# Sign of the converted weights in ScalarE's pass, and one accumulation for the first two units of layer 1

## The chip, the cores and the metric

One NeuronCore of a Trainium2 chip runs the whole program. It has five engines with a queue each: TensorE (PE, with its weight loads as PEld), VectorE (DVE), ScalarE (ACT), GpSimd (POOL) and SyncE (SP), which here only issues transfers. Each engine works through its instructions in the order in which they stand. TensorE reads its operands from SBUF and writes to PSUM, of which there are eight banks of 128 partitions by 512 float32 values. The metric is the device time of one execution in microseconds (us); less is better.

## The reference, cut to what matters

```python
def _attn_ref(q, k, v):                    # (4, 8, 576, 64) each; causal, window of 64
    scores = np.where(mask, scale * np.matmul(q, k.transpose(0, 1, 3, 2)), -1e9)
    attn = np.exp(scores - max); attn = attn / (sum + 1e-09)
    return np.matmul(attn, v)
x = attn_out.transpose(0, 2, 1, 3).reshape(2304, 512)
h = np.maximum(x @ w_in1, 0.0);  x = h * h @ w_out1        # layer 1: 512 -> 2048 -> 512
h = x @ w_in2;                   out = h * np.cos(h) @ w_out2   # layer 2, same sizes
```

The weights of both layers come into the kernel as float64 (their words are seen as pairs of int32), everything else is float32.

## The kernel before, in words

**Products in three parts.** Every float32 operand of the two layers is split into a high and a low part in a type that TensorE multiplies at full rate, and every product is the sum of three: high by high, high by low, low by high. That is why all matmuls of the layers come in groups of three per block of 128 rows, and in groups of twelve for four blocks.

**Units and slices.** The 2304 tokens are cut into nine blocks of 256. Layer 1 works on units: blocks 0, 1 and 2 are units of 256 tokens each, blocks 3 and 4, 5 and 6, 7 and 8 are units of 512 (`spans`, line 415). The 2048 hidden features are cut into 16 slices of 128. An *item* is one unit and one slice: `g1` (line 825) makes the hidden slice in PSUM (tile `ph`, 12 matmuls), `UnitA.act` (line 593) applies relu and square and splits the result (tile `g`: relu, square and square again on ACT, the subtraction on DVE), and `g2` (line 621) adds the slice's share to the unit's output (tile `accA`, 12 matmuls) two items later (`LAG`). So TensorE alternates: `ph` of item i, `accA` of item i-2, `ph` of item i+1, and so on. A matmul's moving operand has as many columns as the unit has tokens, 256 or 512. The outputs leave PSUM through a small ring of two buffers (`x2`) and go to DRAM; layer 2 (`UnitB`, 512 tokens a unit) reads them back.

**Start.** TensorE's first work is attention for block 0, since unit 0 needs its result as input `X`; attention for later blocks is spread between the items. In one group of attention, TensorE makes the scores (`S`), DVE masks and takes the maximum (`mm`, L484), ACT takes the exponential (`pb`, L490), DVE normalises (L496, L497, L500), TensorE transposes (`T`), ACT or DVE copies (`PT`, or `pb` itself in the group of block 1 that borrows a weight buffer), TensorE multiplies by the values (`O`), and ACT and DVE split the result into `X` (L557, L560). Units 0 and 1 are run in turns, item by item, with unit 1 two slices behind (lines 807 to 810), so that a new slice of weights is needed only every second item.

**Converting a slice of weights** (`convert_w`, line 264) turns 128 by 1024 float64 values into float32: ACT scales the high words as if they were float32 (`c0`, by 2^-112) and the low words (`c1`); DVE shifts the high words left by three bits (`c2`, L298), puts the sign bit in (`c3`, L301), and adds the low words (`c4`, L306). For layer 1, ACT then makes the high part (`c5`) and DVE the low part (`c6`, L327), and the slice can be used. For layer 2 the float32 result is stored to DRAM (`w2_dram`) while layer 1 runs, and is read back and split later.

**What sets the order.** All work is recorded as operations with a key, the engines that may do it, a cost on each, and what it depends on. `Plan.run` (line 103) is a list scheduler: it gives out operations engine by engine in the order of its own estimated times (keys break ties within 0.03 us), also choosing the engine where two are allowed, and the instructions are written in that order. Only the order survives; on the chip the queues run at the chip's speed. A changed cost or key therefore can move instructions anywhere behind it. Transfers are issued by SP, in its own planned order.

The lines that the change touches are 283 to 315 (conversion), 415 (`spans`), 621 to 630 (`g2`), 804 to 816 (the list of items and the items at which attention is recorded), 885 (the key's position `pos`) and 915.

Of the kernel before, what the change touches and what calls it, by code (L numbers as in the profile page):

```python
# [9 lines left out]
F32 = mybir.dt.float32  # L10
# [169 lines left out]
def kernel(  # L180
# [83 lines left out]
    def convert_w(src, j, key, after=None, dst=None, early=None):  # L264
# [3 lines left out]

        nm = f"{src.tensor.name}_{j}"
# [14 lines left out]
        def c0(e):  # L284
            hw = words()[1].bitcast(F32)
            copy(e, hw, hw, 2.0**-112)
# [13 lines left out]
        def c3(e):  # L300
            nc.vector.scalar_tensor_tensor(  # L301
                s["w"], words()[1], -(1 << 31), s["w"], ALU.bitwise_and, ALU.bitwise_or)

# [10 lines left out]
        o3 = op({"DVE": dve_us(2 * DM)}, key, c3, [o2], use=[rb, tb])  # L314
        o4 = op({"DVE": dve_us(2 * DM)}, key, c4, [o3, o1], use=[rb, tb])
# [99 lines left out]
    spans = [(0, 1), (1, 1), (2, 1)] + [(n, 2) for n in range(3, NUA, 2)]  # L415
# [158 lines left out]
    class UnitA:  # L574
# [46 lines left out]
        def g2(self, j, m, t, w):  # L621
            i, k = divmod(m, self.per)
            if j == 0 and k == 0:
                self.acc[i] = ps_acc.tile(
                    [P, self.per, self.w], F32, tag="acc", name=f"accA_{self.n}_{i}")
            for p, (wl, gl) in enumerate(((0, 0), (0, 1), (1, 0))):
                nc.tensor.matmul(  # L627
                    self.acc[i][:, k, :], w[:, 1, wl, m * P:m * P + P], t["g"][:, gl, :],
                    start=(j == 0 and p == 0 and k == 0),
                    stop=(j == NJ - 1 and p == 2 and k == self.per - 1), skip_group_check=True)  # L630
# [7 lines left out]
        def finish(self, key, ends):  # L638
            for i, b_acc in enumerate(self.acc_b):
# [18 lines left out]
                for n in self.parts:  # L658
                    for c in range(c0, c0 + self.per):
                        x2_done[n, c] = o  # L660

# [145 lines left out]
    items = [(units[0], j) for j in range(SK)]  # L807
    for j in range(NJ - SK):
        items += [(units[0], SK + j), (units[1], j)]
    items += [(units[1], j) for j in range(NJ - SK, NJ)]  # L810
    items += [(u, j) for u in units[2:] for j in range(NJ)]
    NA = NSA * NJ
    att_at = {0: [1], 2 * NJ - SK: [2], 2 * NJ: [3, 4]}
    for s in range(3, NSA - 1):
        n, k = spans[s + 1]
        att_at[s * NJ] = list(range(n, n + k))
# [67 lines left out]
    for i in range(len(items) + LAG + 1):  # L884
        pos = float(i - LAG)
# [25 lines left out]
        if d >= 0 and i != NA + LAG:  # L911
            g2(d, pos, gs.pop(d))
            k, odd = divmod(d - (NA - NJ), 2)
            if 0 <= k < NJ // 2 and odd:
                reload_w2(k, NA - NJ + 2.4 * k, w2_done[2 * k] + w2_done[2 * k + 1] + [gate])
# [64 lines left out]
```

## Time and profile before

| | |
|---|---|
| three runs, median (lowest to highest) | 894.70 us (893.42 to 894.98) |
| the profiled execution, its own time | 894.97 us |
| its span, first to last instruction | 893.2 us |
| PE busy | 867.7 us of the span, 5424 matmuls |
| DVE, ACT busy | 546.0 us, 474.8 us |
| the part before the last matmul of `accA` for item 1 | 53.44 us |

The profiled execution took 894.97 us, 1.77 us more than its span. An engine's busy time counts a matmul to its modelled end, so that two back-to-back matmuls overlap in the list; the spacing of their starts is what TensorE spends on each. The column PEclk is the clock that TensorE was granted: 1.00 is 2.4 GHz, 0.50 is 1.2 GHz.

### The profile page before, as it was taken

The page shows a single profiled execution, that of the slowest core. Times are in us where ns is not written, and L with a number is a line of the kernel's source. Part 1 is how long each engine was busy: PE and PEld are TensorE (multiplying, and loading weights), DVE is VectorE, ACT ScalarE, POOL GpSimd, SP SyncE. Part 2 cuts the span into 40 slices and gives each one's busy share as a digit, 9 for nine tenths or more (in the row PEclk, how much of TensorE's full clock was granted, in tenths as well). Part 3 has the DMA queues.
Part 4 walks back from the last instruction along what each step waited for, and adds up shares of the span by engine and source line. Part 5 has one row for each costly group of instructions (what it writes and reads, how often), then busy time and mean ns, then how long its engine had stood idle before and what let it go on. Part 6 is the DMA issues. An engine that isn't in the chain of part 4 may idle for free.

```text
span 893.2 us, 13884 instructions
## 1 busy us (share of the span) xinstructions
PE 867.7 (97%) x5424; PEld 741.5 (83%) x5424; DVE 546.0 (61%) x1182; ACT 474.8 (53%) x980; POOL 5.0 (1%) x25
## 2 busy tenths in 40 slices
PE   5699999999999999999999999999999999999998
PEld 4499999998788878888888888888888888888897
DVE  4999956644454345433644976667656666766665
ACT  6979977666556566554434533343334433433444
POOL 2000000000000000000000000000000000000000
PEclk8789999999999999999999999999999999999999
DMA  8753234523533254314542200020002000200010
GB/s 333 295 208 150 72 125 157 184 95 122 192 137 130 75 189 151 139 71 142 176 154 95 72 24 0 1 84 12 1 0 83 12 1 0 71 1 1 8 41 23
DMA packets 23169, 85.43 MB, mean 96 GB/s; under 512 B 2368, under 2 KB 4416, under 8 KB 19008
## 3 DMA queue, kind: packets, MB, share of 16 engines
q1 hardware_dynamic: 23104, 84.55, 26.3%
q8 instruction: 42, 0.69, 0.3%
q14 instruction: 23, 0.19, 0.1%
HBM read 66.72 MB, written 17.83 MB: 95 GB/s over the span
## 4 chain that ended last, share of the span: by engine, by line
PE 91%; DVE 4%; ACT 3%; DMA 1%; issue 1%; SPq 0%; ACTq 0%; DVEq 0%
PE ph L837 42%; PE accB L771 22%; PE accA L627 20%; PE S L471 2%; PE O L522 2%; PE T L508 2%; ACT raw_in_w_dram L245 1%; DMA raw_in_w_dram<-in_w_dram 1%; DVE cw_in_w_dram L301 1%; DVE W_in_w_dram L327 1%; DVE pb L484 0%; DVE pb L500 0%; ACT W_in_w_dram L245 0%; DMA qk<-in_qk_dram 0%; ACT g L604 0%
## 5 line engine op out<-in xcount | busy, mean ns | idle before, releaser
L837 PE MATMUL ph<-X,W_in_w_dram 128*128 128x256 f32 (+1 forms) x1152 | 225.0, 343 | 1.6 <-DVE W_in_w_dram L327 1.6
L627 PE MATMUL accA<-g,W_in_w_dram 128*128 128x256 f32 (+1 forms) x1152 | 222.1, 339 | 0.0
L837 PE MATMUL ph<-X,W 128*128 128x512 f32 (+1 forms) x960 | 209.8, 368 | 0.0
L771 PE MATMUL accB<-W,gb 128*128 128x512 f32 x864 | 208.8, 390 | 0.0
L837 PEld LDWEIGHTS ph<-X,W_in_w_dram 128*128 128x128 f32 x1152 | 182.0, 192 | 26.7 <-DVE W_in_w_dram L327 2.1
L627 PEld LDWEIGHTS accA<-g,W_in_w_dram 128*128 128x128 f32 x1152 | 180.9, 191 | 23.2 <-issue 0.7
L837 PEld LDWEIGHTS ph<-X,W 128*128 128x128 f32 x960 | 169.3, 188 | 31.2
L771 PEld LDWEIGHTS accB<-W,gb 128*128 128x128 f32 x864 | 161.0, 188 | 32.9 <-ACT gb L748 0.2
L721 ACT ACTIVATE u<-ph,quarter 128x512 f32<-128x512 f32 (+1 forms) x80 | 51.7, 646 | 148.8 <-PE ph L837 148.8
L613 DVE TENSOR_TENSOR g<-r,g 128x256 fp32r<-128x256 f32 (+1 forms) x96 | 53.1, 555 | 94.3 <-ACT r L608 93.8
L725 DVE TENSOR_SCALAR u<-u 128x512 f32<-128x512 f32 (+1 forms) x80 | 32.0, 400 | 121.2 <-ACT u L721 121.2
L604 ACT ACTIVATE g<-r 128x256 fp32r<-128x256 f32 (+1 forms) x96 | 50.4, 525 | 77.8 <-PE accA L627 77.3
L748 ACT ACTIVATE gb<-rr 128x512 fp32r<-128x512 f32 (+1 forms) x80 | 47.2, 590 | 83.6 <-DVE rr L743 83.6
L600 ACT ACTIVATE r<-ph 128x256 f32<-128x256 f32 (+1 forms) x96 | 46.5, 484 | 54.5 <-PE ph L837 54.2
L245 ACT ACTIVATE raw_in_w_dram<-raw_in_w_dram 128x1024 f32<-128x1024 f32 x64 | 72.8, 1158 | 3.7 <-DMA raw_in_w_dram<-in_w_dram 3.7
L490 ACT ACTIVATE pb<-pb,mm 128x128 f32<-128x128 f32 x144 | 55.9, 390 | 16.4 <-DVE mm L484 16.4
L740 ACT ACTIVATE u<-rr,hpi 128x512 f32<-128x512 f32 (+1 forms) x80 | 53.7, 672 | 0.3 <-DVE rr L736 0.2
L729 DVE SCALAR_TENSOR_TENSOR rr<-u,ph 128x512 f32<-128x512 f32 (+1 forms) x80 | 50.7, 634 | 2.5
L743 DVE TENSOR_TENSOR rr<-ph,u 128x512 f32<-128x512 f32 (+1 forms) x80 | 50.4, 630 | 1.4 <-ACT u L740 1.3
L751 DVE TENSOR_TENSOR gb<-rr,gb 128x512 fp32r<-128x512 f32 (+1 forms) x80 | 50.5, 631 | 1.0 <-ACT gb L748 1.0
L733 DVE SCALAR_TENSOR_TENSOR rr<-u,rr 128x512 f32<-128x512 f32 (+1 forms) x80 | 50.4, 630 | 0.3
L608 ACT ACTIVATE r<-r 128x256 f32<-128x256 f32 (+1 forms) x93 | 48.8, 524 | 3.0
(61 smaller groups left out, 541.9 us busy)
## 6 DMA issues: line engine op xcount, KB each, us to landing
raw_in_w_dram<-in_w_dram SPq DMA_DIRECT2D x32, 1024.0 KB, 7.3
qk<-in_qk_dram SPq DMA_DIRECT2D x18, 576.0 KB, 4.5
v<-in_v_dram SPq DMA_DIRECT2D x18, 512.0 KB, 3.6
w_dram<-cw_in_w_dram SPq DMA_DIRECT2D x16, 512.0 KB, 3.1
w<-w_dram SPq DMA_DIRECT2D x8, 1024.0 KB, 4.8
x_dram<-x SPq DMA_DIRECT2D x18, 256.0 KB, 2.4
out_dram<-o SPq DMA_DIRECT2D x18, 256.0 KB, 2.0
xr<-x_dram SPq DMA_DIRECT2D x16, 256.0 KB, 2.7
```

Source lines behind the costliest of these rows:

```text
L245: nc.scalar.activation(o, i, AF.Copy, scale=scale)
L490: nc.scalar.activation(t["pb"][:, e, r, i], t["pb"][:, e, r, i], AF.Exp, bias=t["mm"][:, e, r, i:i + 1], scale=-1.0, accum_out=t["sm"][:, ...
L604: nc.scalar.activation(t["g"][:, 0], t["r"], AF.Square)
L613: nc.vector.tensor_tensor(t["g"][:, 1], t["r"], f32(t["g"][:, 0]), ALU.subtract)
L627: nc.tensor.matmul(self.acc[i][:, k, :], w[:, 1, wl, m * P:m * P + P], t["g"][:, gl, :], start=(j == 0 and p == 0 and k == 0), stop=(j == ...
L721: nc.scalar.activation(t["u"], ph()[:, 0:w], AF.Identity, bias=quarter, scale=INV_2PI)
L729: nc.vector.scalar_tensor_tensor(t["r"], t["u"], -C1, ph()[:, 0:w], ALU.mult, ALU.add)
L733: nc.vector.scalar_tensor_tensor(t["r"], t["u"], -C2, t["r"], ALU.mult, ALU.add)
L740: nc.scalar.activation(t["u"], t["r"], AF.Sin, bias=hpi)
L751: nc.vector.tensor_tensor(t["g"][:, 1], t["r"], f32(t["g"][:, 0]), ALU.subtract)
L771: nc.tensor.matmul(self.acc[m], t["g"][:, gl, m * P:m * P + P], w[:, 1, wl], start=(j == 0 and k == 0), stop=(j == NJ - 1 and k == 2))
L837: nc.tensor.matmul(t["ph"][:, 0:u.w], wb.tile[:, 0, wl, c * P:c * P + P], u.x(xl, c), start=(c == 0 and k == 0), stop=(c == NCC - 1 and k ...
```

## The change

The scaling pass on ACT (`c0`) becomes a parametric rectifier: positive words are multiplied by 2^-112 as before, negative ones by 2^-112 times -2^32. A negative word thus becomes a positive float32 whose exponent is larger by 32; 32 is bit 5 of the exponent field, that is bit 28 of the word, and the shift by three of `c2` moves it to bit 31, where the sign belongs. `c3` on DVE is left out. This holds for the 16 slices of either layer.

The first two blocks become one unit of 512 tokens, `(0, 2)`. For slices 0 to 5 it is worked by two halves of 256 columns in turns, as units 0 and 1 were (`Half`, items 0 to 11); both halves add into the two ranges of columns of the same four PSUM banks. Slices 6 to 15 (items 12 to 21) are done for 512 tokens at once. There are 22 items where there were 32. Each item's position for the keys is now in the list `place`, since items no longer stand one unit of position apart.

```diff
         def c0(e):
             hw = words()[1].bitcast(F32)
-            copy(e, hw, hw, 2.0**-112)
+            nc.scalar.activation(hw, hw, AF.Prelu, scale=2.0**-112, alpha=-(2.0**32))
...
-        def c3(e):
-            nc.vector.scalar_tensor_tensor(
-                s["w"], words()[1], -(1 << 31), s["w"], ALU.bitwise_and, ALU.bitwise_or)
...
-        o3 = op({"DVE": dve_us(2 * DM)}, key, c3, [o2], use=[rb, tb])
-        o4 = op({"DVE": dve_us(2 * DM)}, key, c4, [o3, o1], use=[rb, tb])
+        o4 = op({"DVE": dve_us(2 * DM)}, key, c4, [o2, o1], use=[rb, tb])
...
-    spans = [(0, 1), (1, 1), (2, 1)] + [(n, 2) for n in range(3, NUA, 2)]
+    spans = [(0, 2), (2, 1)] + [(n, 2) for n in range(3, NUA, 2)]
...
-            if j == 0 and k == 0:
+            if j == 0 and k == 0 and self.n > 0:
...
-                    start=(j == 0 and p == 0 and k == 0),
+                    start=(j == 0 and p == 0 and k == 0 and self.n > 0),
...
+    class Half:
+        w = UA
+        groups = NCC
+        group_us = 3 * pe_us(UA)
+
+        def __init__(self, unit, k):
+            self.unit, self.k = unit, k
+            self.act = lambda *a: UnitA.act(self, *a)
+
+        def x(self, hl, c):
+            return self.unit.x(hl, c)[:, self.k * UA:self.k * UA + UA]
...
+        def g2(self, j, m, t, w):
+            acc, first = self.unit.acc, j == 0 and self.k == 0
+            if first:
+                acc[m] = ps_acc.tile([P, 1, 2 * UA], F32, tag="acc", name=f"accA_{self.unit.n}_{m}")
+            for p, (wl, gl) in enumerate(((0, 0), (0, 1), (1, 0))):
+                nc.tensor.matmul(
+                    acc[m][:, 0, self.k * UA:self.k * UA + UA],
+                    w[:, 1, wl, m * P:m * P + P], t["g"][:, gl, :],
+                    start=(first and p == 0), stop=False, skip_group_check=True)
...
-    items = [(units[0], j) for j in range(SK)]
-    for j in range(NJ - SK):
-        items += [(units[0], SK + j), (units[1], j)]
-    items += [(units[1], j) for j in range(NJ - SK, NJ)]
-    items += [(u, j) for u in units[2:] for j in range(NJ)]
-    NA = NSA * NJ
-    att_at = {0: [1], 2 * NJ - SK: [2], 2 * NJ: [3, 4]}
-    for s in range(3, NSA - 1):
+    J0 = 6
+    halves = [Half(units[0], k) for k in range(2)]
+    items = [(halves[0], j) for j in range(SK)]
+    for j in range(J0 - SK):
+        items += [(halves[0], SK + j), (halves[1], j)]
+    items += [(halves[1], j) for j in range(J0 - SK, J0)]
+    place = [float(i) for i in range(2 * J0)]
+    items += [(units[0], j) for j in range(J0, NJ)]
+    place += [2.0 * j + 1 for j in range(J0, NJ)]
+    NA = len(items) + (NSA - 1) * NJ
+    items += [(u, j) for u in units[1:] for j in range(NJ)]
+    place += [2.0 * NJ + k for k in range(len(items) - len(place) + LAG + 1)]
+    N2 = NJ + J0
+    att_at = {0: [1], N2 - 4: [2], N2: [3, 4]}
+    for s in range(2, NSA - 1):
...
-        pos = float(i - LAG)
+        pos = place[i] - LAG
```

How the change moves instructions, at three places. In the names, `raw_in_w1_dram_1` is the raw slice 1 of layer 1, `cw_` its sum in the making, `W_` the finished slice; `S_1_1_0`, `T_1_1_0` and `O_1_1` belong to attention for block 1, second group.

DVE at the start, from the shift of slice 1 on; first before, then with the change.

```order
L298 TENSOR_SCALAR cw_in_w1_dram_1_379<-raw_in_w1_dram_1_209 128x1024
L301 SCALAR_TENSOR_TENSOR cw_in_w1_dram_1_379<-raw_in_w1_dram_1_209,cw_in_w1_dram_1_379 128x1024
L327 TENSOR_TENSOR W_in_w1_dram_0_381<-raw_in_w1_dram_0_128,W_in_w1_dram_0_381 128x2x512
L560 TENSOR_TENSOR X_83<-O_1_0_383,X_83 128x2x256
L306 ISA raw_in_w1_dram_1_209<-raw_in_w1_dram_1_209,cw_in_w1_dram_1_379 128x1024x2
L298 TENSOR_SCALAR cw_in_w1_dram_2_440<-raw_in_w1_dram_2_255 128x1024
```

```order
L299 TENSOR_SCALAR cw_in_w1_dram_1_372<-raw_in_w1_dram_1_209 128x1024
L249 COPY PT_1_0_360<-T_1_0_1_374 128x512
L323 TENSOR_TENSOR W_in_w1_dram_0_370<-raw_in_w1_dram_0_128,W_in_w1_dram_0_370 128x2x512
L303 ISA raw_in_w1_dram_1_209<-raw_in_w1_dram_1_209,cw_in_w1_dram_1_372 128x1024x2
L299 TENSOR_SCALAR cw_in_w1_dram_2_415<-raw_in_w1_dram_2_255 128x1024
L557 TENSOR_TENSOR X_83<-O_1_0_382,X_83 128x2x256
L303 ISA raw_in_w1_dram_2_255<-raw_in_w1_dram_2_255,cw_in_w1_dram_2_415 128x1024x2
L323 TENSOR_TENSOR W_in_w1_dram_1_420<-raw_in_w1_dram_1_209,W_in_w1_dram_1_420 128x2x512
```

The sign pass is gone, and slice 2 is summed and slice 1 finished before the maxima of attention for block 1 (second group) begin; before, these stood behind the shift of slice 2, and slices 1 and 2 were finished after them.

TensorE from the scores of attention for block 1 (second group; their last row first) to the first accumulation; first before, then with the change.

```order
L471 MATMUL S_1_1_1_421<-qk_1_1_242 64x128 x2
L837 MATMUL ph_0_408<-X_83,W_in_w1_dram_0_381 128x256 x6
L837 MATMUL ph_1_468<-X_83,W_in_w1_dram_1_438 128x256 x9
L508 MATMUL T_1_1_0_485<-ident_80,pb_1_1_419 128x128 x4
L837 MATMUL ph_1_468<-X_83,W_in_w1_dram_1_438 128x256 x3
L508 MATMUL T_1_1_1_506<-ident_80,pb_1_1_419 128x128 x4
L522 MATMUL O_1_1_517<-pb_1_1_419,v_1_1_306 64x64 x16
L837 MATMUL ph_2_542<-X_83,W_in_w1_dram_2_514 128x256 x12
L627 MATMUL accA_0_0_558<-g_0_490,W_in_w1_dram_0_381 128x256 x6
L627 MATMUL accA_0_1_568<-g_0_490,W_in_w1_dram_0_381 128x256 x6
L837 MATMUL ph_3_579<-X_83,W_in_w1_dram_0_381 128x256 x12
```

```order
L468 MATMUL S_1_1_1_426<-qk_1_1_242 64x128 x2
L877 MATMUL ph_1_457<-X_83,W_in_w1_dram_1_420 128x256 x12
L877 MATMUL ph_2_488<-X_83,W_in_w1_dram_2_452 128x256 x9
L505 MATMUL T_1_1_0_504<-ident_80,pb_1_1_424 128x128 x4
L877 MATMUL ph_2_488<-X_83,W_in_w1_dram_2_452 128x256 x3
L685 MATMUL accA_0_0_519<-g_0_445,W_in_w1_dram_0_370 128x256 x3
L685 MATMUL accA_0_1_526<-g_0_445,W_in_w1_dram_0_370 128x256 x3
L685 MATMUL accA_0_2_531<-g_0_445,W_in_w1_dram_0_370 128x256 x3
L505 MATMUL T_1_1_1_537<-ident_80,pb_1_1_424 128x128 x4
L685 MATMUL accA_0_3_544<-g_0_445,W_in_w1_dram_0_370 128x256 x3
L877 MATMUL ph_3_549<-X_83,W_in_w1_dram_0_370 128x256 x6
L519 MATMUL O_1_1_559<-pb_1_1_424,v_1_1_306 64x64 x16
```

The hidden slice 2 and the first accumulation now stand ahead of `O_1_1`; before, they stood behind it, between it and `ph_3`, the first work that needs its result.

ACT at the same time, from the scaling of the next raw slice on; first before, then with the change.

```order
L245 ACTIVATE raw_in_w1_dram_3_344<-raw_in_w1_dram_3_344 128x1024 x2
L245 ACTIVATE W_in_w1_dram_1_438<-raw_in_w1_dram_1_209 128x2x512
L490 ACTIVATE pb_1_1_419,sm_1_1_449<-pb_1_1_419,mm_1_1_448 128x128 x8
L600 ACTIVATE r_0_483<-ph_0_408 128x256
L604 ACTIVATE g_0_490<-r_0_483 128x256
```

```order
L245 ACTIVATE W_in_w1_dram_1_420<-raw_in_w1_dram_1_209 128x2x512
L597 ACTIVATE r_0_443<-ph_0_403 128x256
L601 ACTIVATE g_0_445<-r_0_443 128x256
L605 ACTIVATE r_0_443<-r_0_443 128x256
L287 ACTIVATE raw_in_w1_dram_3_344<-raw_in_w1_dram_3_344 128x1024
L245 ACTIVATE W_in_w1_dram_2_452<-raw_in_w1_dram_2_255 128x2x512
L487 ACTIVATE pb_1_1_424,sm_1_1_455<-pb_1_1_424,mm_1_1_454 128x128 x8
```

The exponentials of attention for block 1 (second group) stood right behind the high part of slice 1; now the activation of item 0, a scaling pass and the high part of slice 2 stand between.

## Rows read from the trace of the kernel before

**Rows 1.** The page, part 1: busy time, share of the span, instructions
```profile
PE 867.7 (97%) x5424; PEld 741.5 (83%) x5424; DVE 546.0 (61%) x1182; ACT 474.8 (53%) x980; POOL 5.0 (1%) x25
```

**Rows 2.** Busy time by stretch: its length, PE, PEld, DVE, ACT, POOL, PEclk, DMA
```profile
30.87:53.44 22.57, 18.43 (x146) 16.46 (x145) 20.12 (x42) 18.19 (x38) 0.00 (x0) 0.73 0.52 210
53.44:203.05 149.61, 147.30 (x1490) 144.12 (x1490) 106.35 (x246) 118.09 (x285) 0.00 (x0) 1.00 0.41 151
203.05:893.20 690.15, 686.23 (x3578) 568.23 (x3576) 400.26 (x819) 317.59 (x597) 0.00 (x0) 1.00 0.20 71
```

**Rows 3.** Waits of PE from 53.44 to the end: all of them
```profile
PE O L522 <- ACT PT L245: 2.3, 2, 1.2
```

**Rows 4.** Timeline of PE, around 57 and 437: start, length, instructions
```profile
56.00 1.60 PE L627 MATMUL accA<-g,W_in_w_dram 128*128 128x256 f32 x12
57.44 1.60 PE L837 MATMUL ph<-X,W_in_w_dram 128*128 128x256 f32 x12
...
435.95 2.88 PE L837 MATMUL ph<-X,W_in_w_dram 128*128 128x512 f32 x12
438.67 2.88 PE L627 MATMUL accA<-g,W_in_w_dram 128*128 128x512 f32 x12
```

**Rows 5.** Chain of waits, 20 to 60: the sign pass on it
```profile
24.71 1.22 DVE cw_in_w_dram L301
...
29.55 1.22 DVE cw_in_w_dram L301
...
39.07 1.14 DVE cw_in_w_dram L301
```

**Rows 6.** Timeline of PE in the start
```profile
31.97 1.22 PE L837 MATMUL ph<-X,W_in_w_dram 128*128 128x256 f32 x4 [0.30 <-DVE W_in_w_dram L327]
33.12 1.99 PE L471 MATMUL S<-qk 64*64 64x128 f32 x32
...
43.61 1.97 PE L522 MATMUL O<-pb,v 128*64 128x64 f32 x30 [0.76 <-DVE pb L249]
45.51 3.00 PE L837 MATMUL ph<-X,W_in_w_dram 128*128 128x256 f32 x12
```

**Rows 7.** Timeline of ACT: item 0, right behind the last exponential; a steady stretch
```profile
38.57 0.36 ACT L600 ACTIVATE r<-ph 128x256 f32<-128x256 f32 x1
...
84.14 0.43 ACT L604 ACTIVATE g<-r 128x256 fp32r<-128x256 f32 x1
...
86.23 1.19 ACT L245 ACTIVATE raw_in_w_dram<-raw_in_w_dram 128x1024 f32<-128x1024 f32 x1
87.29 0.43 ACT L604 ACTIVATE g<-r 128x256 fp32r<-128x256 f32 x1
```

**Rows 8.** Groups of ACT and DVE by shape: busy, mean ns of one, idle before
```profile
L740 ACT ACTIVATE u<-rr,hpi 128x512 f32<-128x512 f32 x64 | 45.7, 714 | 0.0
...
L748 ACT ACTIVATE gb<-rr 128x512 fp32r<-128x512 f32 x64 | 40.5, 633 | 73.3 <-DVE rr L743 73.3
...
L245 ACT ACTIVATE raw_in_w_dram<-raw_in_w_dram 128x1024 f32<-128x1024 f32 x32 | 37.0, 1155 | 3.7 <-DMA raw_in_w_dram<-in_w_dram 3.7
...
L557 ACT ACTIVATE X<-O 128x512 fp32r<-128x512 f32 x18 | 10.7, 595 | 7.8 <-PE O L522 7.8
...
L301 DVE SCALAR_TENSOR_TENSOR cw_in_w_dram<-raw_in_w_dram,cw_in_w_dram 128x1024 int32<-128x1024 int32 x32 | 39.1, 1223 | 0.8
...
L306 DVE CUSTOM_DVE_ANT_0 raw_in_w_dram<-raw_in_w_dram,cw_in_w_dram 128x2048 uint16<-128x2048 uint16 x16 | 19.5, 1220 | 0.1
...
L560 DVE TENSOR_TENSOR X<-O,X 128x512 fp32r<-128x512 f32 x18 | 12.3, 685 | 9.2 <-ACT X L557 9.2
```

**Rows 9.** Timeline, 143 to 157: a wait of PE behind a load of weights
```profile
153.60 1.11 ACT L245 ACTIVATE raw_in_w_dram<-raw_in_w_dram 128x1024 f32<-128x1024 f32 x1 [1.54 <-DMA raw_in_w_dram<-in_w_dram]
...
155.24 1.15 PE L522 MATMUL O<-PT,v 128*64 128x64 f32 x30 [1.12 <-ACT PT L245]
```

**Rows 10.** The loads of raw weights (line 275): time to landing
```profile
DMA to landing us min/median/max: 4.8/7.3/13.5
```

More of the change, by code (lines that the diff above doesn't have):

```diff
@@ L660, in finish, with x_ready, x_use, g2_bufs @@
                         x2_done[n, c] = o
+    class Half:
[7 more added lines that the diff above has]
+            return self.unit.x(hl, c)[:, self.k * UA:self.k * UA + UA]
+        def x_ready(self, c):
+            n = self.unit.n + self.k
+            return [x_hi[n, c], x_lo[n, c]]
+        def x_use(self):
+            return []
+        def g2(self, j, m, t, w):
[7 more added lines that the diff above has]
+                    start=(first and p == 0), stop=False, skip_group_check=True)
+        def g2_bufs(self, j, m):
+            b = [self.unit.acc_b[m]]
+            return (b, []) if j == 0 and self.k == 0 else ([], b)
     class UnitB:
@@ L806 @@
     SK = 2
-    items = [(units[0], j) for j in range(SK)]
-    for j in range(NJ - SK):
-        items += [(units[0], SK + j), (units[1], j)]
-    items += [(units[1], j) for j in range(NJ - SK, NJ)]
-    items += [(u, j) for u in units[2:] for j in range(NJ)]
-    NA = NSA * NJ
-    att_at = {0: [1], 2 * NJ - SK: [2], 2 * NJ: [3, 4]}
-    for s in range(3, NSA - 1):
+    J0 = 6
[13 more added lines that the diff above has]
+    for s in range(2, NSA - 1):
         n, k = spans[s + 1]
-        att_at[s * NJ] = list(range(n, n + k))
+        att_at[N2 + (s - 1) * NJ] = list(range(n, n + k))
     w2_at, done = {}, 0
@@ L914 @@
             if 0 <= k < NJ // 2 and odd:
-                reload_w2(k, NA - NJ + 2.4 * k, w2_done[2 * k] + w2_done[2 * k + 1] + [gate])
+                reload_w2(k, place[NA] - NJ + 2.4 * k, w2_done[2 * k] + w2_done[2 * k + 1] + [gate])
     with tc.manual_schedule():
```

## The prediction

> **What bounds the kernel now.** I read the busy times first: PE is busy for 97% of the span, no other engine for more than 61% [rows 1]. That is an average, so I cut the span where TensorE's behaviour changes [rows 2]. From 53.44 us on, PE is busy 147.30 of 149.61 us and then 686.23 of 690.15 us, nearly the whole rest of which lies behind its last matmul. The waits confirm it: from 53.44 to the end PE waits 2.3 us, two waits of an `O` on the copy of `PT` by ACT [rows 3]. So after 53.44 the time is the number of matmuls by their spacing, and work taken from DVE or ACT there is worth nothing beyond those 2.3 us. Before 53.44 it is different: from 30.87 on, PE is busy 18.43 of 22.57 us at a mean clock of 0.73 of full, while DVE is busy 20.12 [rows 2]. The chain of waits through this start runs over DVE, and the sign pass stands on it three times [rows 5]. The reader is to see two regimes: a start in which DVE and ACT set the pace, and 840 us in which TensorE does.
>
> **Term 1, the merged items (-3.2 us).** For slices 6 to 15 two items of 256 columns become one of 512. Each pair had 48 matmuls, 24 of them remain: over ten slices 480 become 240. What one costs is the spacing of starts. Twelve matmuls of 256 columns take 57.44 - 56.00 = 1.44 us, 0.1200 each; twelve of 512 take 438.67 - 435.95 = 2.72 us, 0.2267 each [rows 4]. A pair costs 0.2400, its replacement 0.2267, so 0.0133 is saved 240 times: 3.2 us, all on the path, since this stretch is TensorE's.
> A rule speaks against this size. The Trainium skill (TensorE: Matmul & The Clock Gate, section "Back-to-back issue gap") gives the isolated gap of matmuls at full clock as N/2.4 + 2.5 ns, a fixed part of 2.5 ns where the trace has 13.3. By that rule the term would be 240 times 2.5 ns, 0.6 us, and the gain in the sum 2.6 us less. The trace does not agree with it: its fixed part is five times as large, and the measurement decides.
>
> **Term 2, the sign pass in the start (-3.0 us).** One pass on DVE takes 1.22 us [rows 8]. Three stand on the chain before 53.44 (1.22, 1.22, 1.14; 3.6 us in all) [rows 5], but what is late next must be followed. Before, `ph_0` began at 30.87, where the stretch of [rows 2] begins, and broke off at 31.97 to wait for slice 0 [rows 6]; now slice 0 is ready by then, so `ph_0` runs through. At 0.25 us a matmul (3.00 for twelve, at half clock [rows 6]) it ends near 33.9, and the scores of block 1 follow near 35.9.
> In the new order ACT has item 0's activation, one scaling pass and one high part ahead of the eight exponentials. A conversion pass advances ACT by 87.29 - 86.23 = 1.06; from one square at 84.14 to the next at 87.29 are two of them and the three passes of an item, which leaves 3.15 - 2.12 = 1.03 for those [rows 7]. So the exponentials begin at 33.9 + 1.0 + 2.1 = 37.0 and, at about 0.39 each, end at 40.1; before, they ended at 38.57, where item 0 begins on ACT [rows 7]: 1.5 us *later*. From that end to the end of `O` there were 43.61 + 1.97 - 38.57 = 7.0 us [rows 6, 7]; a sign pass and a sum pass (1.14 and 1.22 [rows 5, 8]) no longer stand between. `O` ends between 44.7 and, with two more at half clock, 46.7; before, at 45.6.
> The gain comes behind it: before, `ph_2` and the first `accA` (24 matmuls), `ph_3` and the second `accA` (24) filled 45.6 to 53.44. Now the first 24 and half of `ph_3` are done ahead of `O`. What remains is the split of `X`, 0.595 + 0.685 [rows 8], which that work used to cover, and 18 matmuls: 2.2 us at 0.12, 4.3 at half clock. That gives 48.2 to 52.3 for the point of the work that was reached at 53.44: a gain of 1.1 to 5.2 us. I take 3.0, near the middle, since half clock held through much of the stretch before (mean 0.73) [rows 2].
>
> **Term 3, the two waits on `PT` (-2.3 us).** Both belong to a place in the old order [rows 3]. The second came about because ACT, in order, stood 1.54 us before a scaling pass whose load had not landed, with the copy of `PT` queued behind it [rows 9]. In the new order these places no longer exist. I count -2.3 here, and their successors in term 4.
>
> **Term 4, new waits of TensorE (+1.5 us; 0 to 5).** The planner's order is built on its own costs, and ACT runs the denser program. In a pair of half items ACT has three conversion passes and six short ones: 3 x 1.06 + 2 x 1.03 = 5.2 us [rows 7]; TensorE needs 4 x 1.44 = 5.76 [rows 4]. In a merged item it has 3 x 1.06 and three 512-wide passes of at most 0.633 [rows 8], 5.1 us of 5.44. So ACT keeps up but has no room for a late load. Attention for blocks 2 and 3 now falls into the second half of unit 0; the tightest places are there and at the end of unit 0, where the first two raw slices of layer 2 are scaled in ACT's queue. A load lands after 7.3 us in the median and 13.5 at worst [rows 10]. Nearest row for one such wait: 1.12 us [rows 9]. I take one and a part, 1.5; zero if every load is early, 5 if several are late.
>
> **The rectifier pass itself (0).** It has the shape of the copy that it replaces, 1.155 us for 128x1024 [rows 8], with scale and slope as constants. The trace has no rectifier with a slope. Bounds: below, the copy's 1.155, as no pass of this shape is shorter; the nearest dearer neighbour is the sine at 0.714 against 0.633 for a copy of 128x512 [rows 8], 0.08 more; far above, a pass that runs twice, 2.31. I take the copy's. With 0.08 more, ACT's pair of half items is 5.3 of 5.76 and TensorE still sets the pace: 0 to 0.3 us, the latter for the four passes of the start.
>
> **Layer 2's sixteen sign passes, and the new bookkeeping (0).** They lie in stretches where PE never waits on DVE [rows 3]; losing them gains nothing. The order behind unit (2, 1) is the same but for a few neighbours that change places.
>
> **Sum.** -3.2 - 3.0 - 2.3 + 1.5 = -7.0. The profiled execution took 894.97 (span 893.2, and 1.77 outside it), which gives 888.0; it lies 0.27 above the median of the runs, so I predict 887.7.
>
> **Rivals.**
> *ACT takes DVE's place in the start.* For it: the exponentials move 1.5 us later by my own working. If half clock holds to the end and slice 3 is late as well, term 2 is near zero and term 4 near 2: 894.7 - 3.2 - 2.3 + 2 = 891.2. Against it: 24 matmuls really leave the stretch behind `O`.
> *The merged matmuls do not keep the spacing of [rows 4].* Were a merged matmul to take as long as its pair, 0.2400, term 1 would be nothing; half of it gone makes 889.3. For it nothing in this trace, where later units run 512 columns at 0.2267 with the same slices. (The page of the Trainium skill named under term 1 would leave 0.6 of the 3.2, which makes 890.3.)
> *The end of unit 0 gives it back.* Four banks now leave through two staging buffers, where two and two left; in ACT's queue these copies, a raw slice of layer 2 and the activation of unit 2 stand in one line. With a load that lands at 13.5 instead of 7.3 us and the same again at the first slice of layer 2, the waits are 6 to 8 us: 894 to 895, no change. Against it: the copy of `PT` stands ahead of the second raw slice now, not behind it.
> *The rectifier is a dear pass (slower).* If it runs twice over its data, 1.155 us more, ACT needs 6.4 us for a pair of half items against 5.76 of TensorE and about 6.2 for a merged item against 5.44. Over the 16 slices of layer 1 that is 16 x 1.155 = 18.5 us on ACT; it idles 149.6 - 118.1 = 31.5 us in the stretch from 53.44 on [rows 2], but mostly after the last slice of layer 1. I count the start's three passes (3.5) and about half of the rest (7.5): 887.7 + 11 = 899. It decides from about 0.45 us a pass on, where it eats the 7.0. Against it: all passes of one shape in this trace lie within 13% of one another.
>
> **Chances.** Forecast 0.62 (885 to 890.5); ACT in the start 0.18; the spacing 0.03; end of unit 0 0.09, of which 0.07 within 0.2%; dear rectifier 0.08. A measurement here can tell 0.2%, 1.8 us. Faster: 0.62 + 0.18 + 0.03 + 0.01 = 0.84. Same: 0.07. Slower: 0.08 + 0.01 = 0.09. The range for 8 in 10 starts at the low ends of the terms, -3.2 - 5.2 - 2.3 + 0 = -10.7, 884.0, taken in to 884.6, and reaches over the second rival to 892.6.
>
> **What would show each step.** Term 1: items 12 to 21 with 2.72 us from start to start of twelve matmuls, and 336 `accA` of 256 columns left where 576 were. Term 2: no DVE row for the sign, `ph_0` unbroken, and the second `accA` ended near 50 instead of 53.44. Term 3 and 4: the list of PE's waits from there to the end, at 0 to 3 us. Rectifier: a mean near 1.16 us on its line, and two table loads on ACT as before. I am wrong if PE waits on ACT more than 4 us between 50 and 150, or if TensorE stays at half clock past 53.

## The result and the profile after

The changed kernel takes 885.79 us in the median of four runs (885.30 to 886.78), the kernel before 894.18 beside it: a ratio of 0.9905, 95% interval 0.989 to 0.992, that is 8.4 us less. The profiled execution took 886.27 us with a span of 884.5, against 894.97 and 893.2. The difference of the two profiled executions, 8.70 us, is what the rows below divide.

Part 1 of the page of the changed kernel, beside [rows 1]:

```profile
PE 862.2 (97%) x5184; PEld 724.9 (82%) x5184; DVE 509.8 (58%) x1137; ACT 471.1 (53%) x953; POOL 5.0 (1%) x25
```

5424 - 5184 = 240 matmuls are gone, as counted in the prediction. DVE lost 36 us and ACT 4, which nobody would find in the time: shares of the whole span don't say where a microsecond counts. The stretches do. They are cut at the same points of the work as in [rows 2] (from the first matmul of `ph_0` to the end of the second `accA`; from there to the first matmul of 512 columns of the unit of blocks 3 and 4; the rest), with the same columns:

```profile
30.86:49.45 18.59, 15.68 (x146) 14.10 (x146) 15.57 (x38) 16.32 (x37) 0.00 (x0) 0.86 0.93 379
49.45:194.40 144.95, 144.63 (x1251) 129.72 (x1249) 88.71 (x219) 115.19 (x258) 0.00 (x0) 1.00 0.39 133
194.40:884.50 690.10, 686.22 (x3578) 568.37 (x3576) 386.74 (x806) 318.56 (x598) 0.00 (x0) 1.00 0.20 71
```

Beside [rows 2] this gives the whole sum:

| stretch | before | after | difference | of it PE busy | of it PE idle |
|---|---|---|---|---|---|
| start | 22.57 | 18.59 | -3.98 | -2.75 | -1.23 |
| to the unit of blocks 3 and 4 | 149.61 | 144.95 | -4.66 | -2.67 | -1.99 |
| the rest | 690.15 | 690.10 | -0.05 | | |

In the start the number of matmuls is the same (146), so 2.75 us less of busy time is clock: 0.86 of full in the mean where it was 0.73. In the second stretch the clock is full in both, and busy time went with the 239 matmuls that the records have less. The waits of TensorE from 48 us to the end, beside [rows 3], are a single one:

```profile
PE T L505 <- DVE pb L497: 0.3, 1, 0.3
```

The start on TensorE, beside [rows 6]:

```profile
30.86 2.48 PE L877 MATMUL ph<-X,W_in_w_dram 128*128 128x256 f32 x12
33.27 1.10 PE L468 MATMUL S<-qk 64*64 64x128 f32 x32
...
39.52 1.09 PE L505 MATMUL T<-ident,pb 128*128 128x128 f32 x4 [0.42 <-ACT pb L487]
...
41.04 2.06 PE L685 MATMUL accA<-g,W_in_w_dram 128*128 128x256 f32 x9
...
44.53 1.15 PE L519 MATMUL O<-pb,v 128*64 128x64 f32 x32
46.47 0.38 PE L877 MATMUL ph<-X,W_in_w_dram 128*128 128x256 f32 x1 [0.79 <-ACT X L554]
...
48.01 1.60 PE L685 MATMUL accA<-g,W_in_w_dram 128*128 128x256 f32 x12
```

`ph_0` runs through, the first `accA` stands ahead of `O`, `O` ends at 45.68 (before at 45.58), and behind it remain the split of `X` and 18 matmuls. The chain of waits through this stretch, beside [rows 5], has no sign pass; it runs over ACT:

```profile
33.37 0.39 ACT r L597
33.79 0.42 ACT g L601
34.23 0.42 ACT r L605
34.65 1.02 ACT raw_in_w_dram L287
35.68 1.01 ACT W_in_w_dram L245
36.69 2.71 ACT pb L487 x14
39.52 1.09 PE T L505 x4
```

Merged items, beside [rows 4], and the rectifier beside the other raw pass of its shape, beside [rows 8]:

```profile
72.48 2.91 PE L877 MATMUL ph<-X,W_in_w_dram 128*128 128x512 f32 x12
75.23 1.59 PE L685 MATMUL accA<-g,W_in_w_dram 128*128 128x256 f32 x12
...
90.33 2.88 PE L624 MATMUL accA<-g,W_in_w_dram 128*128 128x512 f32 x12
93.05 1.52 PE L877 MATMUL ph<-X,W_in_w_dram 128*128 128x512 f32 x6
```

```profile
L245 ACT ACTIVATE raw_in_w_dram<-raw_in_w_dram 128x1024 int32<-128x1024 uint32 x32 | 36.9, 1153 | 0.0
L287 ACT ACTIVATE raw_in_w_dram<-raw_in_w_dram 128x1024 f32<-128x1024 f32 x32 | 36.7, 1147 | 1.7 <-DMA raw_in_w_dram<-in_w_dram 1.7
```

From start to start, twelve matmuls of 512 take 2.75 us in the first pair of these rows (72.48 to 75.23) and 2.72 in the second (90.33 to 93.05). The rectifier costs what a copy costs.

### The profile page after: what moved, and what is told of

It reads as the page before. It is cut to its first block, busy times and chain, and to the rows that moved or that the text cites. A ratio compares the mean times of both kernels' runs of the same rounds, so it can differ in the third digit from the quotient of the medians.

```text
span 884.5 us, 13320 instructions
## 1 busy us (share of the span) xinstructions
PE 862.2 (97%) x5184; PEld 724.9 (82%) x5184; DVE 509.8 (58%) x1137; ACT 471.1 (53%) x953; POOL 5.0 (1%) x25
## 4 chain that ended last, share of the span: by engine, by line
PE 91%; ACT 6%; DVE 1%; issue 1%; DMA 0%; ACTq 0%
PE ph L877 42%; PE accB L803 22%; PE accA L624 20%; PE S L468 2%; PE O L519 2%; PE T L505 2%; ACT raw_in_w_dram L287 1%; ACT W_in_w_dram L245 1%; ACT raw_in_w_dram L245 1%; ACT g L601 1%; ACT pb L487 1%; ACT r L597 0%; ACT r L605 0%; DMA qk<-in_qk_dram 0%; DVE pb L497 0%
## 5 line engine op out<-in xcount | busy, mean ns | idle before, releaser
L877 PE MATMUL ph<-X,W_in_w_dram 128*128 128x512 f32 (+1 forms) x1032 | 220.6, 360 | 2.5 <-ACT X L554 0.8
L624 PE MATMUL accA<-g,W_in_w_dram 128*128 128x512 f32 (+1 forms) x888 | 200.5, 370 | 0.0
L877 PEld LDWEIGHTS ph<-X,W_in_w_dram 128*128 128x128 f32 x1032 | 172.6, 190 | 32.4 <-issue 1.4
L624 PEld LDWEIGHTS accA<-g,W_in_w_dram 128*128 128x128 f32 x888 | 153.2, 189 | 27.3 <-issue 0.9
L610 DVE TENSOR_TENSOR g<-r,g 128x512 fp32r<-128x512 f32 (+1 forms) x86 | 51.9, 604 | 107.8 <-ACT r L605 107.0
L601 ACT ACTIVATE g<-r 128x512 fp32r<-128x512 f32 (+1 forms) x86 | 48.3, 561 | 80.3 <-PE accA L624 78.9
L597 ACT ACTIVATE r<-ph 128x512 f32<-128x512 f32 (+1 forms) x86 | 44.9, 522 | 51.6 <-PE ph L877 51.4
L605 ACT ACTIVATE r<-r 128x512 f32<-128x512 f32 (+1 forms) x84 | 47.1, 561 | 2.7
L287 ACT ACTIVATE raw_in_w_dram<-raw_in_w_dram 128x1024 f32<-128x1024 f32 x32 | 36.7, 1147 | 1.7 <-DMA raw_in_w_dram<-in_w_dram 1.7
```

The costliest lines, as they stand in the source:

```text
L601: nc.scalar.activation(t["g"][:, 0], t["r"], AF.Square)
L610: nc.vector.tensor_tensor(t["g"][:, 1], t["r"], f32(t["g"][:, 0]), ALU.subtract)
L624: nc.tensor.matmul(self.acc[i][:, k, :], w[:, 1, wl, m * P:m * P + P], t["g"][:, gl, :], start=(j == 0 and p == 0 and k == 0 and self.n > ...
L877: nc.tensor.matmul(t["ph"][:, 0:u.w], wb.tile[:, 0, wl, c * P:c * P + P], u.x(xl, c), start=(c == 0 and k == 0), stop=(c == NCC - 1 and k ...
```

## The experiments

All are timed in five rounds beside the kernel before, whose median was 893.9 to 894.3 us in these rounds. The table gives the medians and what the three stretches of each profiled execution hold, cut as above; the second `accA` ends where the second stretch begins. Experiment 6 is left out of the last three columns, since its rows are cut elsewhere.

| | median | ratio, 95% | second `accA` ends | second stretch | rest |
|---|---|---|---|---|---|
| before | | | 53.44 | 149.61 | 690.15 |
| changed | 885.79 | 0.989 to 0.992 | 49.45 | 144.95 | 690.10 |
| 1 sign only | 890.14 | 0.9943 to 0.9968 | 48.38 | 148.53 | 690.09 |
| 2 merge only | 889.85 | 0.9944 to 0.9971 | 53.05 | 144.48 | 690.07 |
| 3 passes back, all | 892.62 | 0.9984 to 1.0002 | 52.93 | 147.02 | 690.85 |
| 4 passes back, slices 0 to 2 | 887.67 | 0.9921 to 0.9946 | 51.56 | 144.94 | 690.10 |
| 5 passes back, layer 2 | 888.63 | 0.9919 to 0.9944 | 50.29 | 145.79 | 690.92 |
| 6 two ACT passes | 904.74 | 1.0102 to 1.0129 | | | |
| 7 merged from 3 | 886.26 | 0.9899 to 0.9927 | 49.61 | 144.66 | 690.03 |
| 8 merged from 10 | 888.61 | 0.9924 to 0.9951 | 49.38 | 147.19 | 690.13 |
| 9 fillers, changed | 884.51 | 0.9881 to 0.9908 | 47.62 | 144.98 | 690.10 |
| 10 fillers, before | 892.80 | 0.9978 to 0.9995 | 52.16 | 149.31 | 690.13 |
| 11 layer 2's, planned | 886.10 | 0.9902 to 0.9929 | 48.42 | 144.89 | 690.09 |
| 12 fillers, merged from 4 | 883.67 | 0.9869 to 0.9897 | 47.34 | 144.14 | 691.12 |

### 1 and 2: each part alone

In the kernel before, the rectifier without the merge (1); in the changed kernel, copy and sign pass as before (2).

```diff
 # 1, in the kernel before
-            copy(e, hw, hw, 2.0**-112)
+            nc.scalar.activation(hw, hw, AF.Prelu, scale=2.0**-112, alpha=-(2.0**32))
-        o3 = op({"DVE": dve_us(2 * DM)}, key, c3, [o2], use=[rb, tb])
-        o4 = op({"DVE": dve_us(2 * DM)}, key, c4, [o3, o1], use=[rb, tb])
+        o4 = op({"DVE": dve_us(2 * DM)}, key, c4, [o2, o1], use=[rb, tb])
 # 2, in the changed kernel: these lines the other way round
```

> The kernel before with the rectifier and without the sign pass; units 0 and 1 stay apart for all 16 slices. Up to about 60 us its queues stand in the order of the changed kernel. Theory (start 4.0, merge 3.2, old waits on PT 2.0, each by its own part): the start's 4.0 us are gained, the second accA ends near 49.5, no merged item, the waits of TensorE behind 53 are 0 to 3 us: 888 to 891 us, that is 3.5 to 6 below the kernel before. Rival (the merge does it; without it ACT, with three passes and six short ones a pair, gives the start's gain back later): 893 to 895.

> The changed kernel with the plain scaling copy and the sign pass put back as an operation of its own; units 0 and 1 merged from slice 6 on. Up to about 55 us its queues stand in the order of the kernel before. Theory: the second accA ends near 53.4 as before, the merged items gain 3.2, and the two old waits on PT go or not: 889 to 891 us, 3.2 to 5.5 below the kernel before. With the first experiment the gains add to 8 to 9. Rival (merged items keep DVE or ACT too busy, so that the 3.2 shows only where the sign pass is gone): 893 to 894.5.

Measured: 890.14 and 889.85, 3.8 and 4.1 us below the kernel before in the same rounds; together 7.9, against 8.4 for both at once. Both are where the theory put them. Busy time by stretch, with the columns of [rows 2], of experiment 1 and then of experiment 2:

```profile
31.75:48.38 16.63, 13.34 (x145) 11.91 (x145) 15.52 (x38) 16.15 (x37) 0.00 (x0) 1.00 0.94 382
48.38:196.91 148.53, 147.31 (x1490) 143.89 (x1489) 92.20 (x233) 117.78 (x284) 0.00 (x0) 1.00 0.38 135
```

```profile
30.66:53.05 22.39, 18.06 (x145) 16.09 (x145) 20.15 (x42) 18.22 (x38) 0.00 (x0) 0.74 0.52 212
53.05:197.53 144.48, 144.48 (x1250) 130.16 (x1249) 106.82 (x239) 112.20 (x252) 0.00 (x0) 1.00 0.42 156
```

Without the merge the second stretch stays at 147.31 us of busy time; without the rectifier the start stays at 22.39. So the start is the sign pass's part and the 2.7 us of busy time the merge's. The two old waits on `PT` vanish in either: in experiment 2 no wait at all is left, in experiment 1 one of 1.2 us on another transpose takes their place. They belonged to one order, and both of these other orders lose them.

Experiment 1's queues stand in the changed kernel's order up to some 60 us. Yet in its profiled execution TensorE was at full clock through the whole stretch, where the changed kernel's was at half from 30 to 32 us and again from 40 to 42, and it began 0.89 us later and ended 1.07 earlier. So the clock in this start differs from one execution to the next; the median of experiment 1 lies 1.3 us above its profiled run. Six profiled executions have these queues in one order to beyond 55 us (the changed kernel and experiments 1, 5, 7, 8 and 11), and in them the second `accA` ends between 48.38 and 50.29. A start that is read from a single execution is uncertain by about 1 us either way.

### 3, 4 and 5: the passes put back in the same order

One line more in the operation of the shift, without telling the planner, so that all queues stand as in the changed kernel. The extra pass has the old one's form and length.

```diff
             nc.vector.tensor_scalar(s["w"], words()[1], 3, None, ALU.logical_shift_left)
+            # 3: always; 4: if dst is None and j < 3; 5: if dst is not None
+            nc.vector.scalar_tensor_tensor(
+                s["w"], words()[1], -(1 << 31), s["w"], ALU.bitwise_and, ALU.bitwise_or)
```

> The changed kernel with all its queues in the same order, and behind each of the 32 shifts on DVE one more pass of the old sign pass's form (its sign bit is zero by then, so it changes nothing). Theory (the passes themselves cost in the start, on the chain; later they are hidden): 1.2 to 3.6 us above the changed kernel, 887 to 889.4, all of it before the second accA, which ends at 50.6 to 53. Rival A (the gain in the start is the new order's, not the pass's): within 0.5 us of the changed kernel, 885.5 to 886.5. Rival B (DVE also needed the 29 later passes gone): more than 3.6 above, 890 or more, with waits of TensorE on DVE behind 53.

> As the third experiment, but the extra pass only on slices 0, 1 and 2 of layer 1. Theory: the same time as the third experiment within 0.5 us, 887 to 889.4. Rival B: nearer to the changed kernel than to the third experiment by the price of the 29 later passes, 1 us or more below it. Rival A: 885.5 to 886.5.

> The changed kernel in the same order, with the extra DVE pass of the third experiment only on the 16 slices of layer 2. The prediction put these passes at nothing: 885.3 to 886.3, the changed kernel's time. Rival, read from the third experiment's trace (three sections of attention between 208 and 310 us grew by 0.25 each, one step of 0.8 before 170): 886.6 to 887.6, and no listed wait of TensorE on DVE above 0.5 us.

Three passes in the start cost 887.67 - 885.79 = 1.9 us, by the profiled executions 51.56 - 49.45 = 2.1, and nothing behind it; no run of the one (887.12 to 888.39) lies among those of the other (885.30 to 886.78). But all 32 cost 6.8. That is rival B; the theory that only the start's count fell. Where the rest lies can be read. On DVE, the pass of slice 3 (third experiment) stands in the queue ahead of the low half of `X`:

```profile
48.90 1.23 DVE L300 SCALAR_TENSOR_TENSOR cw_in_w_dram<-raw_in_w_dram,cw_in_w_dram 128x1024 int32<-128x1024 int32 x1
50.05 0.69 DVE L559 TENSOR_TENSOR X<-O,X 128x512 fp32r<-128x512 f32 x1
```

and TensorE waits for that half 1.74 us, where it waited 0.46:

```profile
50.79 0.86 PE L879 MATMUL ph<-X,W_in_w_dram 128*128 128x256 f32 x5 [1.74 <-DVE X L559]
```

Behind the start, a transpose waits 1.4 us on an activation. Experiment 5 has the passes of layer 2 alone. Its median, 888.63, is 2.8 us above the changed kernel's and above both expected ranges, but not all of that is theirs: in its profiled execution the second `accA` ends 0.84 us later than in the changed kernel, and the first of these passes begins at 121.67. Its runs reach from 886.38 to 889.02, and two of the five lie within the changed kernel's. Behind the start the passes cost 0.84 us in the second stretch and 0.82 in the rest (144.95 and 690.10 in the changed kernel), and experiment 3, which has them too, loses 0.75 in the rest. The rows of experiment 5:

```profile
50.29:196.08 145.79, 145.10 (x1251) 129.91 (x1249) 93.22 (x223) 115.21 (x258) 0.00 (x0) 1.00 0.38 132
196.08:887.00 690.92, 686.67 (x3578) 568.00 (x3576) 400.32 (x818) 318.54 (x598) 0.00 (x0) 1.00 0.20 71
```

The prediction put these sixteen passes at nothing, by waits that the kernel before didn't have. Experiment 5 seems to deny it, so it was asked once more.

### 11: layer 2's passes as a planned operation

```diff
+        o3 = o2
+        if dst is not None:
+            o3 = op({"DVE": dve_us(2 * DM)}, key, c3, [o2], use=[rb, tb])
-        o4 = op({"DVE": dve_us(2 * DM)}, key, c4, [o2, o1], use=[rb, tb])
+        o4 = op({"DVE": dve_us(2 * DM)}, key, c4, [o3, o1], use=[rb, tb])
```

> The changed kernel with an extra DVE pass of the sign pass's form on the 16 slices of layer 2, as in the fifth experiment, but as an operation that the planner knows and prices, so that the order is made with it; up to about 85 us the queues are as in the changed kernel. The fifth experiment's passes cost 1.6 us in an order that was made without them. If a replanned order hides them, as the kernel before did: 885.5 to 886.5, and the three sections of attention behind 203 us take 19.9 each. Rival (there is no room for them on DVE wherever they stand): 887 to 888.

886.10 us, as expected, and the second stretch and the rest take what they take without the passes:

```profile
48.42:193.31 144.89, 144.63 (x1250) 129.77 (x1249) 93.53 (x224) 114.85 (x257) 0.00 (x0) 1.00 0.38 137
193.31:883.40 690.09, 686.23 (x3578) 568.24 (x3576) 400.56 (x819) 317.80 (x597) 0.00 (x0) 1.00 0.21 71
```

DVE does the same 400 us of work as in experiment 5, and TensorE loses nothing. So both readings hold: a pass that the order knows is free, and the same pass put into an order that was made without it costs 0.1 us (1.66 for sixteen, by the profiled executions). Putting a pass back without replanning measures the order's slack, not the worth of the removal.

### 6: what a dear rectifier would have cost

```diff
             nc.scalar.activation(hw, hw, AF.Prelu, scale=2.0**-112, alpha=-(2.0**32))
+            copy(e, hw, hw, 1.0)
```

> The changed kernel in the same order, with a second pass on ACT (a copy times 1.0, in place) right behind each rectifier pass: the price of a rectifier that would run twice over its data. By the prediction's rival (three passes of the start and about half of the other thirteen's 15 us reach TensorE): about 11 us above the changed kernel, 895 to 899, with waits of TensorE on ACT's activation and on converted slices between 50 and 150 us. If ACT's 34 idle us from 53 to 203 take them up, only the start pays: 888.5 to 890.5. If each reaches the path: 16 x 1.155 more, 904.

904.74, 18.9 us above the changed kernel: the last of the three cases, about 16 x 1.155 = 18.5, every pass of layer 1. The prediction's rival had it at 11. ACT's idle time took up next to nothing, because it lies where no slice of layer 1 is converted: in the changed kernel ACT is busy 59.26 of the 60.55 us from 49.45 to 110, in which the last of these slices is summed (at 105), and 55.93 of the 84.40 from there to 194.40. Waits of DVE from 50 to 170 us show how the delay goes on, and a row of TensorE its largest step:

```profile
DVE cw_in_w_dram L300 <- ACT raw_in_w_dram L245: 15.9, 12, 1.6
...
108.64 1.08 PE L506 MATMUL T<-ident,pb 128*128 128x128 f32 x4 [6.18 <-DVE pb L498]
```

This transpose waits 6.18 us, where it waited 0.32 in the changed kernel, and the clock fell to half in that wait (0.68 from 104 to 106 us, 0.50 from 106 to 110). The profiled execution, at 902.81, is 16.5 us above the changed kernel's. So the nearness to sixteen passes holds for the median as a whole and isn't shown pass by pass.

### 7 and 8: the point where the merge begins

```diff
-    J0 = 6
+    J0 = 3          # 8: J0 = 10
```

> The changed kernel with the halves ending at slice 3 instead of 6, so that 13 slices are merged, not 10. Term 1's slope is 24 x 0.0133 = 0.32 us a slice: 0.96 less than the changed kernel, 884.8. Rival (the halves' longer items are what lets ACT and the loads catch up behind the start: 5.76 us of TensorE a slice for 5.2 of ACT against 5.44 for 5.1): waits of TensorE on ACT or on a load between 50 and 90 us take it back, 885.8 or more.

> The changed kernel with the halves ending at slice 10, so that 6 slices are merged: 4 x 0.32 = 1.28 more than the changed kernel, 887.1; its queues are the same up to about 55 us. Rival (the merge's worth is in the order it gives to ACT and attention, not in TensorE's spacing): off this by more than 1 us, with other waits of TensorE between 60 and 170.

Both medians miss the theory, 886.26 for 884.8 and 888.61 for 887.1, and lie where the rivals put them. The second stretch of experiment 7, then that of experiment 8:

```profile
49.61:194.27 144.66, 143.99 (x1179) 126.14 (x1178) 88.16 (x216) 114.29 (x249) 0.00 (x0) 1.00 0.39 133
```

```profile
49.38:196.57 147.19, 145.93 (x1347) 135.24 (x1345) 91.11 (x226) 115.45 (x267) 0.00 (x0) 1.00 0.39 131
```

From slice 10 on: 1.30 us more of busy time for four slices, 0.33 each, and a wait of 1.2 us where there was one of 0.3; 2.8 in the medians. From slice 3 on: 0.64 less of busy time for three slices, 0.21 each, and 0.35 more of idle time; the median is no lower than the changed kernel's. In the busy time the slope has the predicted sign and about its size. The waits move by as much, so that the medians don't show it: one doesn't fall, and the other rises by twice the slope's 1.28.

### 9 and 10: the clock of the start, held by idle work

Of the start's 3.98 us the rows put 2.75 to the clock. To test it, transposes of the identity (the fillers of the table) are added where TensorE waits; their result is overwritten.

```diff
             t["T", e] = pool.tile([P, 2, HB, P], F32, tag=ring, name=f"T_{nm}_{e}")
+            for _ in range({(1, 0, 0): 6, (1, 0, 1): 12, (1, 1, 0): 2}.get((n, g, e), 0)):
+                nc.tensor.transpose(t["T", e][:, 0, 0], ident, ident)
             # 10, in the kernel before: (1, 0, 0): 6, (1, 0, 1): 12, (1, 1, 1): 8
```

> The changed kernel with idle transposes of the identity ahead of three transposes of attention for block 1 (6, 12 and 2 of them, overwritten by the real ones), where TensorE waits 1.19, 2.85 and 0.42 us in the start; nothing else moves. Tests what the granted clock of the start is worth. If the clock sets it (O, the first hidden slice and the transposes ran at half clock from 26 to 33 and from 39 to 43): it stays at full through 26 to 33, O takes 1.15 and not 1.97, twelve ph matmuls 1.5 and not 2.5, and the second accA ends 1 to 2.5 us earlier, at 47 to 48.5: 883.3 to 884.8 us. Rival (ACT and DVE set the start, the clock only fills their waits): 885.3 to 886.5, with longer waits on converted slices. If the fillers themselves delay the transposes: up to 1 us slower, 886.8.

> The kernel before with such idle transposes (6, 12 and 8, the last ahead of the second transpose of the second group of block 1, where TensorE waited 1.77 us); the sign pass stays. Of the start's 4.0 us the traces put 1.3 to shorter waits and 2.7 to the granted clock (the same matmuls in 15.7 us instead of 18.4). If that is right, holding the clock gives the kernel before a good part of the 2.7 without the change: 891.5 to 893 us. Rival (the sign pass on DVE's chain sets the start, and a faster TensorE only waits longer): 893.7 to 894.5.

In the changed kernel `O` and `ph_0` now run at full clock, 1.15 and 1.70 us instead of 1.97 and 2.48 (experiment 9):

```profile
29.09 1.15 PE L521 MATMUL O<-PT,v 128*64 128x64 f32 x30 [0.53 <-DVE PT L249]
30.16 1.70 PE L879 MATMUL ph<-X,W_in_w_dram 128*128 128x256 f32 x12
...
46.19 1.60 PE L687 MATMUL accA<-g,W_in_w_dram 128*128 128x256 f32 x12
```

The second `accA` ends 1.83 us earlier and the median falls to 884.51, inside the range expected. (The changed kernel was timed in other rounds; the two ratios, 0.9895 and 0.9905, have intervals that overlap, so the traces carry this and not the medians.) In the kernel before such idle work gives 1.25 us, also inside. But the clock was worth 2.7 by busy time, and only half of that came. The mean clock of this start was 0.92, so the transposes held it in part only. TensorE was busy 2.24 us less than in the kernel before, the added transposes included, but idle 1.24 us more, since it now waits longer for its slices on DVE. The stretch, and its waits from 28 to 54 us (experiment 10), where the kernel before had 1.6 us of them:

```profile
30.59:52.16 21.57, 16.19 (x154) 14.35 (x152) 20.67 (x43) 18.60 (x39) 0.00 (x0) 0.92 0.55 220
...
PE ph L839 <- DVE W_in_w_dram L327: 4.0, 3, 1.8
```

So the rival is half true. A faster TensorE in the start helps only as far as the conversion keeps up, and the sign pass was part of what it then waits for. The gain of the start is not "a pass" and not "the clock", but the two together: fewer waits, and less time at half clock behind them.

### 12: the idle work and an earlier merge together

Experiment 9 with `J0 = 4`.

> The kernel of the ninth experiment with the halves ending at slice 4 instead of 6. The runs of the ninth experiment lay within 0.1 us, so that term 1's slope can be seen by itself: two more merged slices give 2 x 0.32 = 0.64 us, 883.9. Rival (as in the seventh experiment, where 0.96 showed at the first scores behind the start and was gone 80 us later, in waits of transposes and scores): 884.3 to 884.9, with 0.64 less at the first scores of attention for block 2 and nothing left at the first matmul of 512 columns of the third unit.

883.67 us (883.21 to 884.50), the lowest median of this study: 10.4 us below the kernel before in the same rounds, with an interval of the ratio that ends at 0.9897. The changed kernel's, timed in other rounds, begins at 0.989, so the intervals just overlap, though no run of either lies among the other's. Its second stretch against that of experiment 9:

```profile
47.34:191.48 144.14, 144.02 (x1203) 127.21 (x1201) 88.41 (x217) 114.27 (x252) 0.00 (x0) 1.00 0.40 138
```

144.14 for 144.98: 0.59 less of busy time and 0.25 less of waiting. The busy time has term 1's slope, 0.30 us a slice. In its profiled execution the rest took 691.12, 1.0 more than in experiment 9, lost in steps at the borders of units in layer 2; why was not found. So its profiled execution, 884.42, is no faster than experiment 9's, 884.50; three of its five runs lie 0.7 to 1.2 below it.

## Why the prediction was right, step by step

*What bounds the kernel.* Right. The last 690 us did not move by more than 0.05, and the time came from the start and from TensorE's own work.

*Term 1, the merged items: predicted -3.2, measured -2.67* (busy time of the second stretch, 147.30 to 144.63). The count of 240 was right. The cost of each was mis-sized by a sixth: with the 2.72 us for twelve that was taken from 435.95 us on, the term is 3.2; with the 2.75 of the row at 72.48 it is 240 x (0.2400 - 0.2292) = 2.6. Why twelve take 2.72 in one place and 2.75 in another isn't shown. The Trainium skill's rule for the isolated gap (TensorE: Matmul & The Clock Gate, section "Back-to-back issue gap") would have made it 0.6; no run here bears that out.

*Term 2, the start: predicted -3.0, measured -3.98.* The walk held point for point: `ph_0` ended at 33.3 (33.9), the scores at 34.3 (35.9), the exponentials ran from 36.6 to 39.7 (37.0 to 40.1) and so later than before as forecast, `O` ended at 45.7 (44.7 to 46.7), the second `accA` at 49.45 (48.2 to 52.3). What was off is the clock: I let half clock hold, and it rose to full between 32 and 34 us (a mean of 0.84 there, 1.00 from 34 to 38) and stood there again behind `O`, where the kernel before still ran `ph_2` at half clock [rows 6]. Half clock was also priced a little high: 0.25 us a matmul is the length 3.00 by twelve, but from start to start these twelve took 2.80, 0.233 each. Experiments 1 and 2 show that the gain of the start comes with the sign pass's removal and not with the merge, experiments 9 and 10 what part the clock has in it. The size is one draw: in the six executions of this order the second `accA` ends 3.15 to 5.06 us before the 53.44 of the kernel before.

*Terms 3 and 4, old and new waits: predicted -2.3 and +1.5, measured -2.3 and +0.3.* The direction was right, the price of new waits too high here. Behind the start, experiments 1, 2, 7, 8, 9, 11 and 12 have listed waits of 1.2, 0, 0.7, 1.2, 0.4, 0.3 and 0.2 us: this order is an ordinary one, and 1.5 was above them all.

*The rectifier pass at nothing.* Right: 1147 ns beside 1153 for the other raw pass in the same trace, and 1155 for the copy before [rows 8]. The bound below wasn't one: three passes of this shape in the kernel before (`W` from `w`) took 1056.

*Layer 2's passes at nothing.* Right as a removal (experiment 11), where the kernel before was planned with them; put into an order that was made without them they cost 1.66 us (experiment 5).

*The rivals.* ACT did take DVE's place on the chain, but the 24 matmuls moved ahead of `O` kept the gain. The end of unit 0 cost nothing: the second stretch has 0.3 us of waits in all. The dear rectifier did not come, and its price, 11 us, was wrong: experiment 6 has 18.9. The step that failed there is "about half of the rest"; I counted idle time of ACT over a whole stretch, though it was idle only where no slice was due. The 0.45 us a pass at which this rival would eat the 7.0 counts all sixteen passes (7.0 / 16) and not the nine and a half that it reckons with.

*The sum: predicted -7.0, measured -8.7 in the profiled executions and -8.4 in the medians.* Against the forecast, term 1 gave 0.5 us less, term 2 gave 1.0 more, and the waits took 1.2 less. The mechanism held, but that the sum came this near is in part luck: the misses partly offset each other, and the start varies by about 1 us either way.

## What to carry to other kernels

Cut the trace at the same points of the work in both kernels, and split each stretch into busy and idle time: with the same number of matmuls, a change in busy time is mostly clock, and with the same clock mostly work (not wholly: experiment 5 has 0.47 us more of it in its second stretch, 145.10 against 144.63, with the same matmuls at full clock). A pass off the bounding engine is worth something only where an in-order queue puts it ahead of something awaited, and what it is worth depends on whether the order was made with it. Idle time pays for extra work only if it lies where that work is due.

## What the runs showed of the hardware

The rectifier with a slope of -2^32 and a scale of 2^-112 costs ACT no more than a scaling copy of that shape (1147 against 1153 ns).

The granted clock in the start is not a property of the program alone. Profiled executions whose queues stand in the same order there had a mean of 0.86 (the changed kernel) and 1.00 (experiments 1 and 11). In the changed kernel it fell from full to half between 38 and 42 us, after TensorE had waited 0.41, 0.76 and 0.42 us since 36:

```profile
36.00:38.00 2.00, 0.83 (x5) 0.42 (x4) 1.74 (x7) 2.00 (x8) 0.00 (x0) 1.00 1.02 430
38.00:40.00 2.00, 1.58 (x10) 1.40 (x11) 1.67 (x5) 2.00 (x11) 0.00 (x0) 0.87 1.02 430
40.00:42.00 2.00, 2.00 (x11) 2.00 (x10) 1.26 (x4) 1.36 (x5) 0.00 (x0) 0.50 1.00 422
```

With the transposes of experiment 9 it stayed at 1.00 from 24 us on in the profiled execution, and the second `accA` ended 1.83 us earlier. Idle work in a wait can so be worth a microsecond of real work behind it. That it narrows the spread of the time isn't shown: the four runs of experiment 9 lay within 0.07 us (884.45 to 884.52), where the changed kernel's lay within 1.5, but those of experiment 12, with the same transposes, reach from 883.21 to 884.50, and two of experiment 9's four had a mean clock of 0.993 and 0.994 over the whole execution and were no slower. Why one execution of a given order keeps the clock and another loses it was not settled.
